# Output stores of 128-row tiles: one transfer with a three-dimensional destination in place of two

## The chip, the cores and the metric

The kernel runs on one core of one Trainium2 chip. The metric is device time in microseconds (us), the median of several runs; lower is better. A profile is one further execution, recorded instruction by instruction, with its own span (first to last instruction).

Engines are named as the profile names them: PE (matmul), PEld (PE's weight loads), DVE, ACT, POOL and SP. SP, ACT and POOL start DMA transfers from their instruction queues (SPq, ACTq, POOLq). 16 DMA engines move the data.

## The reference

Attention with a squared ReLU in place of the softmax, and a mixture of low-rank adapters on its output:

```python
scores = (1 / sqrt(64)) * q @ k.T              # q, k, v: 8 batches, 12 heads, 448 rows, 64 wide, f32
attn   = maximum(scores, 0) ** 2 / 448
x      = (attn @ v)                            # heads side by side: x is 3584 x 768
logits = x @ w_gate                            # 8 experts, the best two are kept
w      = softmax of the two kept logits
out    = x + sum over the two: w_e * (x @ A_e) @ B_e      # rank 16
```

The output is 3,584 x 768 float32, 11.01 MB.

## The kernel before

**Tiling.** The attention runs over 8 batches and, in each, three groups of four heads. The 448 rows of a batch are seven blocks of 64 that are strided: block j holds rows j, j+7, j+14 and so on, since a load reads `(p j)` with j inner. For every batch, group and block, PE makes scores (L449, `qk`), ACT or DVE applies the ReLU (L468, L470), DVE squares (L485), PE multiplies with v (L516, `pv`), and ACT or DVE copies the result to `xt` in SBUF as bfloat16 (L544). `xt` holds the transposed x for all 3,584 columns.

**Outputs.** The 3,584 rows make 28 tiles of 128, each two neighbouring blocks of 64. A batch has seven blocks, so tiles 3, 10, 17 and 24 have their first block in one batch and their second in the next. Tiles are gated in groups of three (`gate`, L560 to L639); then `outputs` works on each tile `tl` in two halves of 384 columns: PE makes x and the adapters' part in PSUM (L705 and L714, `b`), ACT or DVE evicts it to the tile's SBUF buffer `osb` (L743, `o`), and a store sends `osb` to `out`. There are four `osb` buffers. For tiles 15 to 23, x comes back by DMA transposes of `xt` into `xb` (L655), issued on SP's queue between the stores, and DVE adds it during the eviction (L734).

**Stores.** `k.out` is the output seen as `b j p f`: batch, block, row within the block, column. A row of 768 float32 is 3,072 bytes, and rows of one block lie 7 x 3,072 bytes apart. `st` (L752) walks over the tile's 128 rows and issues one transfer for each block of 64. Tiles 24 and 26 are stored from ACT's queue, all others from SP's. The last tile, 27, is stored in two halves of 384 columns, one from SP and one from ACT. That is 58 transfers.

**Loads.** q, k and v are loaded by POOL's queue, two transfers of 64 partitions for each tensor, batch and group (L185); a load casts float32 to bfloat16, so a row reads 1,792 bytes and writes 896.

**Order.** The text `ORDER` lists every operation by a short name, with the engine after a colon and the first PSUM bank after an @ sign. `ordered` turns it into the program; each engine gets its instructions in that order, and the framework adds the waits that the data, the buffers and the banks need. In the text `st` is a store (st2 is tile 1), `xb` a transpose of `xt`, `f` a load or another operation without a name of its own.

Of the kernel before, what the change touches and what calls it, by code (L numbers as in the profile page):

```python
# [14 lines left out]
J = 7  # L15
CUT = 3
SPIN = 8
PH = 64
# [11 lines left out]
PARTS = {b: ((0, S, 1),) for b in range(NB)}  # L30
PARTS.update({7: ((0, 320, 1), (320, 448, 4))})


C = dict(late=6, xi=(), om=(), merge_x=0, sqs=(2, 2, 3), xback=(15, 23), xblat=1.4, xbdur=1.35, bx=8, xlag=6, xh=2, apart=3, apcap=1, gl=(3, 1), tqlat=2.0)
# [5 lines left out]
f4 f3 f1 f0 f2 f6 f5 f8 f7 f11 f9 f10 f84@0 f12 f88 f85@2 f90 f89 f13 f87@4 qk0@6 f91 qk1@0 qk2@2 relu0:D qk3@4  # L40
f14 relu1:A relu2:D relu3:A tp2@6 f17 qk4@0 relu4:A te2 qk5@4 qk6@2 sq2 relu5:A tp3@6 f16 f86@0 relu6:A te3 sq0
qk7@0 f15 qk8@4 qk9@6 relu7:A tp4@2 relu8:D relu9:A f18 qk10@0 te4 qk11@4 relu10:A qk12@6 sq4 tp5@2 relu11:A f19
qk13@0 relu12:A te5 tp6@4 f26 relu13:A sq9 qk14@2 qk15@6 tp7 relu14:A f23 sq7 pv0@0 pv1 pv2 relu15:A pv3 qk16@2
te6 pv4 pv5 relu16:A f20 pv6 qk17@6 x13:D pv7@4 relu17:A qk18@2 sq11 pv8 f22 pv9 x12:A qk19@6 relu18:A pv10
qk20@0 relu19:D f21 pv11 relu20:A pv12 pv13 qk21@2 x27:A sq16 qk22@6 f27 qk23@0 relu21:A aw1@5 sq14 relu22:A f33
relu23:A x26:D qk24@2 tp8@6 ae1 f25 relu24:A qk25@0 sq18 qk26@4 tp9 relu25:A f55 pv14@2 pv15 pv16 relu26:A pv17
te8 qk27@0 pv18 f31 pv19 relu27:A pv20 sq23 qk28@4 qk29@6 x41:A f28 qk30@0 relu28:A x40:D aw0@3 sq25 relu29:A
f29 relu30:A qk31@4 tp10@6 ae0 tp11 relu31:A f32 sq21 qk32@0 qk33@2 relu32:A te10 pv21@4 pv22 f30 relu33:A pv23
qk34@0 sq30 qk35@6 relu34:A qk36@2 f37 relu35:D relu36:A qk37@0 pv24 pv25 pv26 relu37:A sq32 qk38@2 f35 tp12@6
pv27 relu38:A tp13 qk39@0 x55:A te12 f43 qk40@2 x54:A z0@5 relu39:A sq35 qk41@6 f34 z1 relu40:A qk42@0 relu41:D  # L50
z2 relu42:A qk43@2 f38 gmax0 relu43:A tp14@6 sq28 qk44@0 tp15 relu44:A f42 qk45@2 gd0 gu0 te14 relu45:A qk46@0
gt0 relu46:A f50 sq39 qk47@6 pv28@2 pv29 pv30 gsg0 pv31 relu47:A qk48@0 f24 pv32 pv33 gw0 sq44 pv34 relu48:A f48
qk49@6 x69:A gzp0 tp18@0 relu49:A tp19 sq37 f36 pv35@4 zt0@3 zt1 zt2 x68:A qk50@6 te18 zT0:A pv36 f41 pv37
relu50:A qk51@2 pv38 sq46 pv39 relu51:A pv40 qk52@0 f47 qk53@6 pv41 relu52:A tp16@2 x82:D tp17 relu53:A te16
qk54@0 b2@4 relu54:A sq49 f44 qk55@6 o2:A qk56@2 qk57@0 relu55:A relu56:D b0@4 f49 x83:A relu57:D qk58@6 o0:A
qk59@2 relu58:A z3@5 z4 f39 sq51 relu59:A qk60@0 qk61@6 z5 sq56 relu60:A b4@4 f40 relu61:A gmax3 qk62@2 sq58
b1@0 relu62:A f46 gu3 gd3 o4:A qk63@6 gt3 sq42 qk64@2 gsg3 o1:A b3@1 f65 relu63:A gw3 b5@4 gzp3 relu64:A sq60
f51 zt3@0 zt4 zt5 o3:A pv42@6 pv43 o5:A qk65@2 st2 pv44 zT3:A pv45 sq53 qk66@4 relu65:A pv46 pv47 pv48 tp20@0
relu66:A st4 qk67@2 tp21 x96:D x97:A f53 te20 pv49@4 relu67:A pv50 qk68@6 st0 pv51 pv52 relu68:A pv53 sq63 f66
pv54 pv55 qk69@0 qk70@2 x110:A relu69:D qk71@6 f45 relu70:A b6@4 relu71:A x111:D qk72@0 o6:D tp22@2 relu72:A  # L60
sq65 qk73@6 tp23 pv56@4 pv57 relu73:A f74 qk74@0 te22 pv58 pv59 relu74:A pv60 qk75@6 f79 pv61 sq67 pv62 relu75:A
qk76@2 b8@0 relu76:A x124:D qk77@6 f64 x125:A sq70 tp24@2 relu77:A tp25 qk78@4 z6@1 te24 f59 relu78:A qk79@6 z7
relu79:A o8:D qk80@4 qk81@2 f52 sq72 z8 relu80:A b10@0 relu81:A gmax6 sq77 f54 qk82@6 tp26@4 o10:A tp27 qk83@2
relu82:A gd6 gu6 b7@0 te26 f56 relu83:A qk84@6 gt6 o7:D qk85@4 gsg6 relu84:A qk86@2 gw6 f70 sq74 b9@0 relu85:A
pv63@6 pv64 relu86:A gzp6 pv65 qk87@4 pv66 sq79 pv67 relu87:A pv68 pv69 zt6@1 zt7 x139:A x138:D zt8 qk88@2 o9:A
qk89@4 zT6:D qk90@6 relu88:A st8 relu89:D tp28@0 tp29 relu90:A qk91@2 f80 te28 pv70@4 pv71 relu91:A pv72 pv73
qk92@6 f60 sq84 pv74 pv75 relu92:A pv76 qk93@0 b14@2 x153:D x152:A f58 relu93:A sq81 qk94@6 tp30@4 o14:A tp31
pv77@0 relu94:A pv78 f77 qk95@2 te30 pv79 pv80 relu95:A pv81 qk96@6 pv82 f57 sq91 pv83 relu96:A qk97@4 b11@2
relu97:D x166:A f67 b12@3 x167:A o11:A sq93 qk98@6 o12:A st10 qk99@0 qk100@4 relu98:A relu99:D b13@2 relu100:A
z9@3 st6 sq88 qk101@6 o13:A tp32@0 qk102@4 relu101:A tp33 b15@2 st12 f62 sq86 relu102:A qk103@6 o15:A te32 f61  # L70
qk104@4 relu103:A z10 z11 sq100 relu104:A qk105@0 f69 pv84@6 pv85 pv86 relu105:A gmax9 qk106@4 pv87 sq95 f72
pv88 relu106:A pv89 pv90 qk107@0 x181:A qk108@4 f63 gd9 gu9 x180:A relu107:D b16@2 relu108:A gt9 qk109@6 o16:D
f81 pv91@0 gsg9 pv92 relu109:A gw9 pv93 sq105 qk110@4 pv94 pv95 relu110:A pv96 f78 qk111@6 gzp9 pv97 relu111:A
x195:D zt9@2 zt10 qk112@4 sq98 x194:A zt11 f75 b17@3 relu112:A zT9:D qk113@6 o17:A sq102 pv98@0 qk114@4
relu113:A pv99 st16 tp36@2 pv100 tp37 relu114:A pv101 qk115@6 te36 pv102 pv103 relu115:A st14 pv104 tp34@4 tp35
f83 sq109 qk116@2 x209:A qk117@6 x208:A b20@1 relu116:A f68 te34 b22@0 relu117:A f71 sq114 o20:A qk118@2 qk119@4
qk120@6 relu118:A b21@1 f73 sq112 o22:A b23@2 relu119:A o21:D z12@3 sq107 relu120:A st20 qk121@0 qk122@4
relu121:A z13 relu122:D z14 o23:A qk123@6 pv105@0 gmax12 pv106 relu123:A qk124@4 gd12 pv107 gu12 pv108 gt12
sq116 pv109 relu124:A pv110 pv111 qk125@6 f82 b18@2 gsg12 relu125:A gw12 x223:D x222:A qk126@4 f76 o18:D qk127@6
relu126:A b19@1 gzp12 sq121 relu127:A zt12@0 zt13 zt14 qk128@2 pv112@4 pv113 o19:D relu128:A qk129@6 pv114  # L80
zT12:D pv115 st18 pv116 relu129:A pv117 sq123 pv118 tp38@2 qk130@0 x236:A tp39 qk131@6 st22 relu130:A b24@4 te38
relu131:A tp42@0 sq119 tp43 x237:A qk132@2 b25@6 relu132:A te42 xb90 b28@7 o24:A o25:A sq128 xb93 qk133@2 o28:A
qk134@4 tp40@0 relu133:A sq126 pv119@6 tp41 pv120 relu134:A pv121 xb91 qk135@2 te40 pv122 pv123 relu135:A pv124
pv125 qk136@4 x251:D xb94 qk137@0 x250:A b29@2 sq130 relu136:A b26@3 st24 relu137:A sq135 o29:A qk138@6 qk139@4
o26:A qk140@0 xb92 z15@2 relu138:A relu139:D z16 z17 relu140:A qk141@6 st28 gmax15 pv126@4 pv127 relu141:A gd15
pv128 gu15 qk142@0 gt15 sq133 pv129 pv130 gsg15 pv131 relu142:A xb108 qk143@6 pv132 gw15 b27@3 gzp15 x264:A
x265:D relu143:A zt15@2 xb111 zt16 zt17 sq137 pv133@0 o27:A qk144@4 tp44@6 zT15:A pv134 tp45 relu144:A xb95
qk145@2 pv135 te44 pv136 relu145:A pv137 qk146@4 pv138 pv139 st26 sq140 relu146:A z18@6 b30@7 x279:A sq142 z19
x278:A xb109 qk147@2 qk148@4 qk149@0 o30 relu147:A z20 sq144 b32@7 relu148:A xb112 relu149:A b33@2 gmax18 xb110
qk150@4 o32 qk151@0 relu150:A b31@3 gu18 o33 relu151:A gd18 qk152@4 sq149 st32 b34@7 relu152:A gt18 o31 gsg18  # L90
qk153@0 qk154@4 gw18 o34 relu153:A b35@2 st30 gzp18 relu154:A qk155@0 o35 pv140@6 relu155:A pv141 sq151 qk156@4
xb113 pv142 pv143 relu156:A qk157@2 qk158@0 pv144 pv145 relu157:D relu158:A pv146 tp46@4 tp47 x293:A x292:D
qk159@0 qk160@2 relu159:A zt18@7 te46 zt19 xb126 zt20 z21@6 relu160:A z22 sq156 zT18:A qk161@0 qk162@4 qk163@2
relu161:A xb129 b40@7 sq147 relu162:A z23 sq158 relu163:A qk164@0 xb127 pv147@4 pv148 pv149 relu164:A pv150
qk165@2 o40 pv151 pv152 relu165:A pv153 sq154 qk166@0 xb130 b41@7 relu166:A gmax21 x307:A gu21 qk167@2 gd21
pv154@0 sq163 x306:A pv155 pv156 st34 relu167:A pv157 pv158 qk168@4 gt21 o41 pv159 gsg21 pv160 b36@2 gw21 x320:A
gzp21 xb128 x321:A b38@3 sq161 relu168:A zt21@7 zt22 sq165 zt23 qk169@0 st40 zT21:A pv161@4 pv162 pv163
relu169:A pv164 qk170@6 o38 pv165 pv166 relu170:A o36 pv167 xb131 b37@3 x335:D x334:A sq168 qk171@0 qk172@6
relu171:A qk173@4 z24@2 o37 z25 relu172:A sq170 st36 b46@3 relu173:A b47@0 o46 b39@1 sq172 b44@3 o47 z26 o39
pv168@6 st46 pv169 pv170@4 gmax24 pv171 x338:A pv172@0 gd24 gu24 pv173 x343:A gt24 x339:A o44 b45@6 gsg24 x346:A  # L100
# [830 lines left out]
```

## Time and profile before

| | us |
|---|---|
| median of 3 runs | 182.09 |
| lowest and highest | 181.49 and 182.18 |
| the profiled execution's own time | 182.88 |
| its span | 180.8 |

The stages of the span, with the busy time of the engines:

| stretch, us | PE | DVE | ACT | POOL | what runs |
|---|---|---|---|---|---|
| 0 to 60 | 50.91 | 52.59 | 53.00 | 52.85 | loads at their densest, attention, no store yet |
| 60 to 120 | 58.53 | 58.83 | 59.48 | 37.09 | loads, attention and the first stores |
| 120 to 165 | 44.89 | 44.24 | 41.28 | 0 | last attention, transposes of xt, stores |
| 165 to 181 | 10.89 | 7.95 | 2.69 | 0 | outputs and stores of the last tiles |

How to read the lines shown further on. The first part of the page gives an engine's busy time, its share of the span and the number of instructions. The chain is the work that ended last, followed backwards from the last instruction; it gives shares of the span. The part on queues gives packets, megabytes and the time that the packets took as a share of 16 DMA engines over the span (q0 is POOL's queue, q1 SP's, q10 ACT's). A line of a tile's view gives the issues of a kind with their shortest, median and longest duration in ns, and when the first and the last started. A line of stretches gives, for each engine, busy time and instructions, then PE's granted clock, the mean busy share of the DMA engines, and GB/s. A line of groups gives count, busy time and mean ns, then the idle time before and what ended it.

### The profile page before, as it was taken

What the parts mean: (1) busy time and instruction counts of PE and PEld (TensorE: products, weight loads), DVE (VectorE), ACT (ScalarE), POOL (GpSimd) and SP (SyncE); (2) the same over time, 40 slices, a digit from 0 to 9 for tenths busy, and PEclk for the clock granted to TensorE, in tenths of its full rate; (3) what the DMA queues carried; (4) which work ended last, traced back from release to release, by engine and by line L of the source; (5) the groups of instructions that cost most, each with busy time, mean ns of one, the idle gap of its engine ahead of it and who ended that gap; (6) DMA issues with size and microseconds to landing.
All of it is one profiled execution on the core that took longest, in us unless ns stands there. A gap on an engine that the chain in (4) does not pass through costs nothing.

```text
span 180.8 us, 7744 instructions
## 1 busy us (share of the span) xinstructions
PE 165.2 (91%) x3366; PEld 99.2 (55%) x3366; DVE 163.6 (90%) x254; ACT 156.4 (87%) x240; POOL 89.9 (50%) x155
## 2 busy tenths in 40 slices
PE   7777889788999999999999899999999999999990
PEld 2434466454555565655646475655666557676640
DVE  0799799999989999999999899999999999999740
ACT  3499899999999999999999999999999899992120
POOL 7998998979669377760877487340000000000000
PEclk9997899999999999999999999999999999999999
DMA  5999999999999999996599999997376579467875
GB/s 94 127 175 180 156 142 179 182 184 164 214 142 146 186 237 194 176 178 141 68 143 287 224 181 259 224 170 202 68 126 144 131 175 110 101 149 176 227 215 172
DMA packets 34450, 30.50 MB, mean 169 GB/s; under 512 B 11952, under 2 KB 30896, under 8 KB 34416
## 3 DMA queue, kind: packets, MB, share of 16 engines
q0 software_dynamic: 22000, 17.03, 64.9%
q1 hardware_dynamic: 11792, 11.90, 26.5%
q10 hardware_dynamic: 624, 1.08, 2.2%
q8 instruction: 26, 0.43, 1.0%
q14 instruction: 8, 0.07, 0.1%
HBM read 33.84 MB, written 11.01 MB: 248 GB/s over the span
## 4 chain that ended last, share of the span: by engine, by line
PE 51%; ACT 27%; POOL 7%; DMA 6%; issue 4%; DVE 3%; ACTq 0%; DVEq 0%; POOLq 0%
ACT a L468 24%; PE ps L714 18%; PE ps L449 11%; PE ps L516 10%; DMA q<-in_q_dram 6%; PE ps L560 4%; PE ps L310 3%; PE ps L705 3%; POOL q L185 3%; POOL k L185 3%; PE ps L622 2%; ACT osb L743 2%; DVE a L485 2%; ACT xt L544 1%; POOL k_rest L216 1%
## 5 line engine op out<-in xcount | busy, mean ns | idle before, releaser
L468 ACT ACTIVATE a<-ps 128x896 bf16<-128x896 f32 (+3 forms) x158 | 132.6, 952 | 3.7 <-PE ps L449 3.1
L485 DVE TENSOR_TENSOR a<-a 128x1792 bf16<-128x1792 bf16 (+3 forms) x75 | 89.0, 1200 | 0.0
L449 PE MATMUL ps<-qT 64*64 64x448 bf16 (+2 forms) x756 | 58.1, 342 | 3.9 <-ACT a L468 2.4
L714 PE MATMUL ps<-B,zT 128*128 128x384 f32 x112 | 47.5, 515 | 0.0
L516 PE MATMUL ps<-a,v 64*64 64x448 bf16 (+2 forms) x756 | 45.3, 335 | 1.6 <-DVE a L485 1.3
L449 PEld LDWEIGHTS <-qT 64*64 64x64 bf16 x756 | 25.1, 105 | 31.8 <-issue 23.2
L185 POOL DMA_DIRECT2D k<-in_k_dram x46 | 27.9, 629 | 18.2 <-PE ps L310 7.3
L185 POOL DMA_DIRECT2D v<-in_v_dram x48 | 29.0, 629 | 6.2 <-PE ps L449 1.8
L185 POOL DMA_DIRECT2D q<-in_q_dram x48 | 29.4, 651 | 4.9 <-DMA v<-in_v_dram 2.7
L516 PEld LDWEIGHTS <-v 64*64 64x64 bf16 x756 | 22.7, 108 | 9.0 <-issue 4.1
L324 DVE COPY qT<-ps 128x1792 bf16<-128x1792 bf16 x21 | 22.8, 1085 | 0.2
L544 ACT CAST xt<-ps 128x448 bf16<-128x448 f32 (+2 forms) x37 | 19.0, 554 | 2.9 <-PE ps L516 2.7
L743 ACT COPY osb<-ps 128x384 f32<-128x384 f32 x26 | 13.1, 523 | 7.1 <-PE ps L714 4.1
L714 PEld LDWEIGHTS ps<-B,zT 128*128 128x128 f32 x112 | 17.3, 190 | 3.3 <-issue 0.3
L470 DVE TENSOR_SCALAR a<-ps 128x896 bf16<-128x896 f32 (+1 forms) x16 | 16.9, 1067 | 0.5 <-PE ps L449 0.5
L310 PEld LDWEIGHTS <-q 64*64 64x64 bf16 x672 | 10.4, 111 | 6.3 <-issue 2.5
L560 PEld LDWEIGHTS <-xt 128*128 128x128 bf16 x168 | 10.5, 98 | 5.8 <-issue 4.7
L560 PE MATMUL ps<-awg,xt 128*128 128x136 bf16 x168 | 13.5, 223 | 0.0
L705 PEld LDWEIGHTS <-xt 128*128 128x128 bf16 x114 | 8.0, 98 | 9.9 <-issue 8.1
L310 PE MATMUL ps<-identb,q 64*64 64x64 bf16 x672 | 10.8, 196 | 2.5 <-DMA q<-in_q_dram 1.3
L705 PE MATMUL ps<-identb,xt 128*128 128x128 bf16 x114 | 12.7, 220 | 0.2
L544 DVE CAST xt<-ps 128x448 bf16<-128x448 f32 (+2 forms) x17 | 9.6, 571 | 2.2 <-PE ps L516 2.2
(47 smaller groups left out, 97.5 us busy)
## 6 DMA issues: line engine op xcount, KB each, us to landing
out_dram<-osb SPq DMA_DIRECT2D x50, 192.0 KB, 3.9
q<-in_q_dram POOLq DMA_DIRECT2D x48, 112.0 KB, 4.8
v<-in_v_dram POOLq DMA_DIRECT2D x48, 112.0 KB, 5.0
k<-in_k_dram POOLq DMA_DIRECT2D x46, 112.0 KB, 5.1
out_dram<-osb ACTq DMA_DIRECT2D x4, 192.0 KB, 2.9
B<-in_moe_B_dram POOLq DMA_DIRECT2D x1, 384.0 KB, 8.0
xb<-xt SPq DMA_TRANSPOSE x18, 3.1
a_raw<-in_moe_A_dram POOLq DMA_DIRECT2D x1, 192.0 KB, 5.2
```

The source lines that it names most:

```text
L185: nc.gpsimd.dma_start(out=t[g * PH : g * PH + PH], in_=k.qkv[w][b, g, :, 2 * q : 2 * q + 2, :])
L310: nc.tensor.transpose(k.ps_b[sl * PH : sl * PH + PH, o.banks[g], (w * J + j) * PH : (w * J + j) * PH + PH], source(w, j)[r, sl], k.identb[ ...
L324: nc.vector.tensor_copy(t.rearrange("p g w x -> p g (w x)"), k.ps_b[:, m.banks[0] : m.banks[0] + 2, : 2 * S])
L449: nc.tensor.matmul(out=bank(o, sl)[g * PH : g * PH + PH, at : at + w], lhsT=t[r, g, 1, j * PH : j * PH + PH], rhs=t[r, g, 0, x0:x1], start ...
L468: nc.scalar.activation(out, flat(qk_ops[n], w), ACTF.Relu, scale=k.relu_scale)
L470: nc.vector.tensor_scalar(out, flat(qk_ops[n], w), k.relu_scale, 0.0, op0=ALU.mult, op1=ALU.max)
L485: nc.vector.tensor_mul(a, a, a)
L516: nc.tensor.matmul(out=bank(head, g)[sl * PH : sl * PH + PH, :w], lhsT=vn[r, sl, j * PH : j * PH + PH], rhs=T["a", g0][r, x + sl * width(n ...
L544: evac(w, lambda cp, g=g: cp(k.xt[:, g * QUADS + q, b * S + x0 : b * S + x1], bank(src, g)[:, :w]), deps=[pv_ops[n]], free=[(src, g)], key ...
L560: nc.tensor.matmul(out=bank(zops[0])[:, t * ZW : t * ZW + ZW], lhsT=k.xt[:, do, 128 * tiles[t] : 128 * tiles[t] + 128], rhs=k.awg[:, do, : ...
L705: nc.tensor.matmul(out=out(h)[:, x * 128 : x * 128 + 128], lhsT=k.xt[:, 3 * h + x, c0 : c0 + 128], rhs=k.identb, start=(x == 0), stop=Fals ...
L714: nc.tensor.matmul(out=o, lhsT=T["zT", g0][:, zi], rhs=rhs, start=xb is not None, stop=True, skip_group_check=True,)
```

## The change

A tile whose two blocks lie in one batch is stored by one transfer: its source is the whole tile of 128 partitions, its destination the two blocks, `k.out[b0, j0 : j0 + 2]`, which is a pattern of 2 blocks x 64 rows x 768 columns. A tile that lies in two batches keeps its two transfers. The halves of tile 27 become one transfer each (2 x 64 x 384).

```diff
+        (b0, j0), (b1, j1) = (divmod((c0 + r) // PH, J) for r in (0, PH))
+
         def st(e, c1=0, c2=2 * W):
-            r = 0
-            while r < 128:
-                b, x = divmod(c0 + r, S)
-                j, p = divmod(x, PH)
-                m = min(PH - p, 128 - r)
-                if b >= c["bx"]:
-                    j = TURNED[j]
-                {"SP": nc.sync, "ACT": nc.scalar, "POOL": nc.gpsimd}[e].dma_start(
-                    out=k.out[b, j, p : p + m, c1:c2], in_=T["osb", tl][r : r + m, c1:c2])
-                r += m
+            dma = {"SP": nc.sync, "ACT": nc.scalar}[e].dma_start
+            if b0 == b1:
+                dma(out=k.out[b0, j0 : j0 + 2, :, c1:c2], in_=T["osb", tl][:, c1:c2])
+                return
+            for i, (b, j) in enumerate(((b0, j0), (b1, j1))):
+                dma(out=k.out[b, j, :, c1:c2], in_=T["osb", tl][i * PH : i * PH + PH, c1:c2])
```

The text `ORDER` is written anew. Each engine's sequence of operations, and the sequence of stores and transposes on SP's queue, is the same as before; the words of different engines are interleaved otherwise, and many banks have other numbers. Of 308 takings of a bank, 19 follow another holder than before: six pairs of neighbouring score and transpose takings are exchanged, and so are seven takings among the outputs of the last tiles (b49, b50, b51, b53, b54, b55, zt27):

```diff
-gd27 gu27 o52:A gt27 gsg27 b50@4 gw27 gzp27 o53:D zt27@3 b51@2 st53 b48@5 o51:D b49@0 o50:A o48:D zT27:A st50
-b54@1 o49:A st49 b55@7 o54:D st54 o55:D st55
+z27@0 b52@1 o43 gmax27 st42 gd27 gu27 b53@3 gt27 o52:A gsg27 b50@2 gw27 gzp27 o53:D zt27@4 b51@5 st53 o50:A
+b48@3 o51:D zT27:A st50 b49@2 o48:D b54@3 o49:A st49 b55@2 o54:D st54 o55:D st55
```

The diff also brings options that are left empty here (`om2`, `fl`, `gf`, `sp`, and `sqp`, `tg`, `ai` with the values that were fixed before) and other cost figures for the planner that once made the order; none of them changes an instruction.

## The prediction

> **What bounds the kernel now.** I read the busy shares first, then the chain that ended last, then the DMA queues, then the waits of SP's queue, and last the stretches in which stores run.
>
> ```profile
> PE 165.2 (91%) x3366; PEld 99.2 (55%) x3366; DVE 163.6 (90%) x254; ACT 156.4 (87%) x240; POOL 89.9 (50%) x155
> PE 51%; ACT 27%; POOL 7%; DMA 6%; issue 4%; DVE 3%; ACTq 0%; DVEq 0%; POOLq 0%
> ```
>
> Three engines are busy for some nine tenths of the span, and the chain runs through PE and ACT. The 6% of DMA in it is the first load of q; no store stands in the chain. So today stores cost nothing but the last one's landing: the last eviction is over at 176.5 us (0.56 us from 175.92) and the span ends at 180.8.
>
> ```profile
> L760 SPq DMA_DIRECT2D out_dram<-osb x52: 466/588/1845, 61.9 to 176.2; - x52
> L760 ACTq DMA_DIRECT2D out_dram<-osb x6: 473/575/626, 171.7 to 177.0; - x6
> DMA to landing us min/median/max: 2.6/3.4/7.7
> ```
>
> 58 stores leave between 61.9 and 177.0 us, each 0.59 us of issue. SP is not short of time: it waits for its work, as the longest wait in SP's own list shows.
>
> ```profile
> SPq L760 <- ACT osb L743: 85.5, 4, 60.7
> ```
>
> The queues say how much of the 16 DMA engines the stores take, and how they are spread.
>
> ```profile
> q0 software_dynamic: 22000, 17.03, 64.9%
> q1 hardware_dynamic: 11792, 11.90, 26.5%
> q10 hardware_dynamic: 624, 1.08, 2.2%
> ```
>
> q10 is ACT's queue. Its 624 packets are 512 rows (one 64-row load, four stores of 64 rows, two half stores of 64) and 112 closing records. 112 is 7 x 16: each of its seven transfers closed on all 16 engines, so a 64-row store puts 4 rows on each. The same count fits the loads. The price of bytes on one engine is also here: 2.2% of 16 x 180.8 us is 63.6 us for 1.08 MB, 0.18 us for a 3,072-byte row, with the waiting for other queues in it. The trace's packet records give the undisturbed value: 119 ns at the least, and a row each 0.12 us where a ring has its engine for itself.
>
> ```profile
> 62.00:83.00 21.00, 20.48 (x483) 12.31 (x475) 20.94 (x31) 21.00 (x32) 13.05 (x22) 1.00 1.12 192
> 106.00:124.00 18.00, 17.96 (x438) 11.12 (x428) 17.63 (x26) 17.87 (x28) 9.05 (x16) 1.00 1.12 218
> 133.00:148.00 15.00, 15.00 (x247) 8.67 (x250) 14.59 (x32) 14.05 (x24) 0.00 (x0) 1.00 0.65 138
> ```
>
> The number before the last is the DMA share. It is about one while loads run, so no DMA engine has room then; after the loads it is 0.65.
>
> ```profile
> L185 POOL DMA_DIRECT2D v<-in_v_dram x26 | 15.6, 614 | 5.0 <-PE ps L449 1.8 <-DMA q<-in_q_dram 1.7 <-DMA k<-in_k_dram 0.6
> L185 POOL DMA_DIRECT2D q<-in_q_dram x18 | 10.9, 626 | 3.1 <-DMA v<-in_v_dram 2.7 <-DMA k<-in_k_dram 0.3
> L185 POOL DMA_DIRECT2D k<-in_k_dram x18 | 10.8, 612 | 14.4 <-PE ps L310 7.3 <-PE ps L449 6.9
> ```
>
> Those are the loads issued from 62 to 131 us: 62 of them are still to come when the first store leaves.
>
> **The change, part by part.** *Issues.* Tiles 3, 10, 17 and 24 straddle two batches and keep two transfers. The other 23, and the two halves of tile 27, lose one issue each: 58 become 33. That is 25 x 0.59 = 15 us of queue time, 23 issues of it on SP, which idles anyway: worth nothing. On ACT the store of tile 26 (two issues from 171.66 us) held up the eviction o50, and the last half is two issues ending at 177.6; one fewer there could end the run some 0.5 us sooner.
>
> *Banks.* Every engine's instructions stay in their order, but 19 of 308 bank takings follow another holder. Twelve are swaps inside a pair of score or transpose takings, and only exchange the waits of neighbours. In the tail b49, b54 and b55 now wait for the evictions o50, o48 and o49. By the rows of before o48 (173.32 plus 0.56) is over at 173.88 and b54's first matmul starts at 173.99; o49 is over at 174.67 and b55 starts at 174.85. b49 starts at 173.12 and o50 ends at 173.50, 0.4 us too late, but one issue fewer ahead of it on ACT brings it to 172.9. So zero, and 0.4 us if that issue isn't saved; behind b49 stand b54, b55 and the last stores. The cover is the half tile of matmuls (0.87 us) between two takings.
>
> *Bytes and landing.* The bytes and rows are the same. What is new is the shape: a destination of 2 x 64 rows against a source of 128 partitions, where both sides had 64. No row of before shows how a transfer whose outermost count is 2 is divided. The ends are all 16 engines (8 rows each, 1.0 us by 0.12 us a row) and two engines, one for each index of that dimension: 64 rows each, 64 x 0.12 = 7.7 us. I take two, because the only division that any transfer here shows, q10's seven, is an equal cut of an outermost count that 16 divides on both sides, and of a count of 2 such a cut gives two shares; for a finer one the engine would have to cut the next dimension, which nothing shows.
>
> The Trainium skill has a rule against this change. "DMA: Bandwidth & Descriptors", in the section "Why a DMA increments its semaphore by 16 and not by 1", says that the number of engines is the largest up to 16 that divides the slowest count of both access patterns, and its "Rules for kernel authors" say that an outermost size under 16 confines the whole transfer to that many engines. By it 128 against 2 is two engines, the lowest-numbered two each time, and the sum is the one below. The same list also advises one 128-partition transfer in place of two halves, as they share the engines anyway; by that line alone the time would be that of the first rival. No run shown so far decides between the two.
>
> *The sum with two engines.* All merged stores go through the same two engines, so their work is counted there, from the first store. 24 tiles (23, and tile 27 as two halves) x 64 rows x 0.12 = 184 us. Four straddling tiles, eight transfers of 4 rows on each engine: 8 x 4 x 0.12 = 4 us. Loads: 62 x 128 rows over 16 engines is 8 rows each, 496 rows. By the page a packet of q0 takes 64.9% of 16 x 180.8 us over 22,000, 0.085 us; as the share goes to 1.12, they overlap a little: 0.08, so 40 us. Transposes: the records show 6,912 pieces of 18 ns, 432 on an engine: 8 us. First store issued 61.9 plus 0.6 to its first row: 62.5. Together 62.5 + 184 + 4 + 40 + 8 = 298.5, and about 1.5 from the last row to the span's end (179.3 to 180.8 in before): a span of 300. The profiled execution had a span of 180.8 and a time of 182.88; the median is 182.09, 1.3 over the span. Forecast **301 us**.
>
> Why nothing hides it: from 62.5 to 177 us there are 115 us for 236 us of work. With only four osb buffers, the eviction of tile t+4 waits until tile t has landed; it stands in the order of ACT or DVE, the relus behind it wait, and then PE's scores. Loads wait too, since each has an eighth of its rows on those two engines, and alternate there with the stores; so do the transposes, on which DVE's additions from tile 15 on wait. The point from which this decides: on n engines a store's share is 24 x 128 x 0.12 / n = 369/n us, and beside 40 and 8 us of other work 115 us leave 67, so under about 5.5 engines.
>
> *Ends.* If loads, transposes and landing gaps cost nothing and a row takes 119 ns: 62.5 + 183 + 1.5 + 1.3 = 248. If a row takes 0.18 us, the mean of q10 with its waits, which then stand for the loads: 24 x 64 x 0.181 = 278, in all 62.5 + 278 + 1.5 + 1.3 = 343. I take the value near the undisturbed row plus the loads on their own, since with 14 engines idle between there is little else to wait for.
>
> **Rivals.** *Divided over 16 engines, nothing on the path (the other side).* For it: the builder may be free to cut 2 x 64 as 128 rows, as it keeps the same rows in the same order. Then landing grows from the second half's 3.4 us by at most the 0.5 us of four more rows, less the issue saved. Tail minus 0.5 us: 181.6 us. Chance 0.12. It decides wherever the cut reaches six engines or more. *The same, with the gain in ACT's tail in full:* o50 one issue (0.6 us) earlier and one issue (0.6 us) less at the end: 182.09 - 1.2 = 180.9. Against it: PE's b matmuls, 0.87 us each half tile, and not ACT, carry the chain's last 5 us. Chance 0.03. *Four engines:* 92 us of store rows, 62.5 + 92 + 4 + 40 + 8 + 2.8 = 209. Nothing speaks for a four but the chance of a cut I don't know: 0.02. *That the merge doesn't happen* is out: the built program's list of instructions has 23 stores of 2x64x768, two of 2x64x384 and the straddlers' eight of 64x768.
>
> **How the numbers follow.** Two engines 0.83, four 0.02, sixteen 0.15. Half a per cent, 0.9 us, is what the runs can tell (the three of before spread over 0.7 us). Slower: 0.85. Faster by over 0.5%: 0.03 of the tail case and 0.01 of the first rival, 0.04. Within: 0.11. The range is that of the forecast's own ends, 248 to 343; it leaves out the sixteen and four, 0.17.
>
> **What would show it.** Right: merged stores close with 2 records in place of 16, so q1 has 11,792 - 23 x 16 - 23 x 14 = 11,102 packets (11,424 if they close on sixteen); issue to landing over 8 us against 3.4; waits of ACT and DVE at the evictions for out_dram; the mean DMA share after the first store falls while the span grows; nothing changes before 62 us. Wrong: landing near 4 us and a span near 180. Right in kind but wrong in size: if the two engines serve loads first, or the transposes leave the two engines idle while DVE waits for them.

## The result and the profile after

The changed kernel takes **306.76 us** (median of 6 runs, 306.56 to 308.36), the kernel before 182.09 us (6 runs beside it, 181.49 to 182.99). The ratio is 1.687, with a 95% interval of 1.6812 to 1.6929: slower by over two thirds. The forecast was 301 us with a range of 248 to 343. Here and below, executions more than 1.5% above the fastest of their kernel are left out of the ratios, though not of the medians; two stood far above, one of the kernel before (299.91 us) and one of experiment 7's second kernel (373.93 us).

The page after, its busy shares, the three rows on the clock and the DMA engines in 40 slices, the queues, and the chain that ended last:

```profile
PE 193.5 (63%) x3366; PEld 109.3 (36%) x3366; DVE 164.9 (54%) x254; ACT 159.6 (52%) x240; POOL 90.2 (30%) x155
...
PEclk9799999999758995997775797975897986555755
DMA  6999999989664786666762196992195111111211
...
q0 software_dynamic: 22000, 17.03, 40.7%
q1 hardware_dynamic: 11102, 11.90, 25.2%
q10 hardware_dynamic: 564, 1.08, 1.1%
...
DMA 11%; DVE 0%; DVEq 0%; issue 0%
DMA out_dram<-osb 11%; DVE osb L770 0%; DVEq L952 0%; DVEq L770 0%
```

No engine is near nine tenths of the span any more. DVE, ACT and POOL do the work of before in nearly the same busy time; PE does the same 3,366 matmuls in 193.5 us where it had 165.2, at a granted clock of 0.804 in the mean (0.988 before), lowest where PE waits most. The queues move the same bytes. q1 has 690 packets fewer: 23 merged stores close with 2 records in place of 32 (23 x 30 = 690). The chain that ended last, 51% PE before, is now a store: 34.6 us from 254.5 us on, then DVE's last eviction. In the DMA row a lone 1 or 2 is two of sixteen engines at work.

The tile view of `osb`, whose columns for an issue are the shortest, median and longest duration in ns:

```profile
L784 SPq DMA_DIRECT2D out_dram<-osb x23: 511/544/7906, 62.0 to 289.7; - x23
L787 SPq DMA_DIRECT2D out_dram<-osb x6: 532/588/9702, 108.5 to 228.9; - x6
...
  DMA out_dram<-osb: 84.2, 11
```

The first store leaves at 62.0 us as before (61.9), and in the 60 us before it each engine's busy time is within 2% of what it was (PE 50.43 us against 50.91). The evictions into `osb` idle 84.2 us for earlier stores; before, that row did not exist.

The waits of the whole span (us in all, times, longest):

```profile
ACT osb L770 <- DMA out_dram<-osb: 49.5, 6, 13.1
...
ACT a L471 <- PE ps L452: 38.2, 28, 5.5
DVE osb L770 <- DMA out_dram<-osb: 32.9, 4, 13.2
...
PEld L313 <- DMA q<-in_q_dram: 15.3, 14, 3.3
...
DVE osb L761 <- DMA xb<-xt: 12.7, 2, 8.1
```

A full `osb` holds ACT and DVE in their order for up to 13 us at a time; besides, PE's transposes of q wait for their loads, the additions for `xb`, and the ReLUs for PE's scores.

Stretches of the span (engine busy times, then PE's granted clock, DMA share, GB/s):

```profile
62.00:83.00 21.00, 15.02 (x417) 9.61 (x406) 16.54 (x24) 15.02 (x21) 8.88 (x15) 0.93 0.79 128
66.00:106.00 40.00, 26.14 (x563) 14.69 (x555) 24.07 (x34) 24.44 (x35) 15.14 (x26) 0.83 0.67 109
255.00:279.00 24.00, 5.75 (x16) 2.90 (x17) 1.48 (x4) 1.23 (x4) 0.00 (x0) 0.50 0.13 52
```

The last of them is the plainest line of the trace. A share of 0.13 is 2.1 engines of 16, and 52 GB/s is what they moved: 26 GB/s each. The packet records of the same 24 us hold 407 store rows of 3,072 bytes, 0.118 us a row on each of two engines. Of these rows 128 are ACT's, the store of tile 26 that was issued at 259.7 us; they are sent among SP's, from 263.7 us on, and the rate stays that of two engines. So the merged stores of both queues go through the same two, as the prediction's sum assumed. In the stretch from 66 to 106 us they hold 437 store rows and 3,278 load rows. That is 5.5 store rows per us on each of the two engines, and 5.1 load rows on each of sixteen, if the loads are spread evenly: about one for one.

### The profile page after: what moved, and what is told of

Its sections match the earlier page's. It is cut to its first block, busy times and chain, and to the rows that moved or that the text cites. A ratio compares the mean times of both kernels' runs of the same rounds, so it can differ in the third digit from the quotient of the medians.

```text
span 305.6 us, 7703 instructions
## 1 busy us (share of the span) xinstructions
PE 193.5 (63%) x3366; PEld 109.3 (36%) x3366; DVE 164.9 (54%) x254; ACT 159.6 (52%) x240; POOL 90.2 (30%) x155
## 3 DMA queue, kind: packets, MB, share of 16 engines
q1 hardware_dynamic: 11102, 11.90, 25.2%
## 5 line engine op out<-in xcount | busy, mean ns | idle before, releaser
L734 PE MATMUL ps<-B,zT 128*128 128x384 f32 x112 | 57.9, 614 | 15.1 <-DVE osb L761 15.0
L452 PE MATMUL ps<-qT 64*64 64x448 bf16 (+2 forms) x756 | 63.4, 368 | 5.2 <-ACT a L471 2.7
L519 PE MATMUL ps<-a,v 64*64 64x448 bf16 (+2 forms) x756 | 53.1, 372 | 7.9 <-DVE osb L761 3.9
L770 ACT COPY osb<-ps 128x384 f32<-128x384 f32 x26 | 12.6, 502 | 53.0 <-DMA out_dram<-osb 49.5
L519 PEld LDWEIGHTS <-v 64*64 64x64 bf16 x756 | 25.5, 120 | 20.0 <-issue 13.0
L725 PE MATMUL ps<-identb,xt 128*128 128x128 bf16 x114 | 14.6, 245 | 26.2 <-ACT osb L770 14.2
L770 DVE COPY osb<-ps 128x384 f32<-128x384 f32 x12 | 6.6, 555 | 44.9 <-DMA out_dram<-osb 32.9
L734 PEld LDWEIGHTS ps<-B,zT 128*128 128x128 f32 x112 | 21.0, 228 | 19.4 <-DVE osb L761 15.5
L761 DVE TENSOR_TENSOR osb<-ps,xb 128x384 f32<-128x384 f32 x18 | 9.7, 552 | 33.3 <-issue 18.5
L725 PEld LDWEIGHTS <-xt 128*128 128x128 bf16 x114 | 9.2, 109 | 40.1 <-issue 39.0
L313 PE MATMUL ps<-identb,q 64*64 64x64 bf16 x672 | 12.6, 205 | 12.9 <-DMA q<-in_q_dram 11.2
```

Of the source, the lines that this page charges most:

```text
L313: nc.tensor.transpose(k.ps_b[sl * PH : sl * PH + PH, o.banks[g], (w * J + j) * PH : (w * J + j) * PH + PH], source(w, j)[r, sl], k.identb[ ...
L452: nc.tensor.matmul(out=bank(o, sl)[g * PH : g * PH + PH, at : at + w], lhsT=t[r, g, 1, j * PH : j * PH + PH], rhs=t[r, g, 0, x0:x1], start ...
L519: nc.tensor.matmul(out=bank(head, g)[sl * PH : sl * PH + PH, :w], lhsT=vn[r, sl, j * PH : j * PH + PH], rhs=T["a", g0][r, x + sl * width(n ...
L725: nc.tensor.matmul(out=out(h)[:, x * 128 : x * 128 + 128], lhsT=k.xt[:, 3 * h + x, c0 : c0 + 128], rhs=k.identb, start=(x == 0), stop=Fals ...
L734: nc.tensor.matmul(out=o, lhsT=T["zT", g0][:, zi], rhs=rhs, start=xb is not None, stop=True, skip_group_check=True,)
L770: cp(osb()[:, h * W : h * W + W], out(h)[:, :W])
```

## The experiments

Each ran beside the kernel before on the same chip, whose medians in the four sets were 181.69 us (experiments 1 to 3), 182.12 (4, 5 without the sixteen, and the six tiles of 7), 182.61 (6 with four buffers, and the first set of 7's two tiles) and 181.36 (the rest).

**1. The change without its merge.** New `ORDER`, new banks, two transfers for every tile.

```diff
-            if b0 == b1:
-                dma(out=k.out[b0, j0 : j0 + 2, :, c1:c2], in_=T["osb", tl][:, c1:c2])
-                return
```

> The changed kernel with its two transfers of 64 rows put back for every tile; its new order text and banks stay. Theory (two DMA engines carry each merged store): 182.1 us, within 0.9, q1 again 11,792 packets, stores landing in about 4 us. Rival (the bank takings that follow another holder, or the rewritten order, cost something): 185 us or more, with waits at the last b matmuls.

181.35 us (12 runs), ratio 0.9994 (0.9963 to 1.0024). q1 has 11,792 packets and stores land in 3.3 us at the median. The whole slowdown comes with the merged transfers; order and banks are worth nothing that can be measured.

**2. The merge, with 64 as the outermost count.** The same number of transfers, the same rows in each, the destination written as 64 x 2 rows.

```diff
-                dma(out=k.out[b0, j0 : j0 + 2, :, c1:c2], in_=T["osb", tl][:, c1:c2])
+                dma(out=k.out[b0, j0 : j0 + 2, :, c1:c2].rearrange("j p f -> p j f"), in_=T["osb", tl][:, c1:c2])
```

> The changed kernel with the two dimensions of the merged destination exchanged: 64 x 2 rows in place of 2 x 64, still one transfer of 128 rows of 3,072 bytes to the same two blocks; the rows of a tile go to each other's places in the output. Theory (the outermost count alone sets the number of engines): 16 closing records for each merged store, q1 11,424 packets, landing about 4 us, 181.1 to 182.5 us. Rival (a transfer of twice the size is what blocks the queue and the buffers): 8 us or more to land and 250 us or more, as in the changed kernel.

181.52 us (12 runs), ratio 1.0001 (0.9961 to 1.0041). Its page and the tile view of `osb`:

```profile
q1 hardware_dynamic: 11424, 11.90, 22.6%
...
out_dram<-osb SPq DMA_DIRECT2D x22, 384.0 KB, 3.6
```

```profile
L784 SPq DMA_DIRECT2D out_dram<-osb x23: 538/554/1338, 62.8 to 177.2; - x23
...
DMA to landing us min/median/max: 2.7/3.4/7.6
```

The packets are those that the prediction gave for a close on sixteen engines, 11,424, and landing is that of before. So neither three dimensions nor 384 KB in one transfer cost anything: the outermost count of 2 does. The run also shows what a merge is worth where it is spread well: 25 issues fewer, and no time gained.

**3. The gain at the end alone.** The kernel before, with only the halves of tile 27 stored by one 64 x 2 transfer each. The last copies of x are written with the two blocks' columns interleaved, so that every row keeps its place in the output.

```diff
+        last = (b, u) == (NB - 1, 1)
+
+        def two(x):
+            return x.rearrange("p (r j) -> p j r", j=2) if last else x
+
+        def one(x):
+            return x.rearrange("p (j r) -> p j r", j=2) if last else x
...
-            evac(w, lambda cp, g=g: cp(k.xt[:, g * QUADS + q, b * S + x0 : b * S + x1], bank(src, g)[:, :w]),
+            evac(w, lambda cp, g=g: cp(two(k.xt[:, g * QUADS + q, b * S + x0 : b * S + x1]), one(bank(src, g)[:, :w])),
...
+            if tl == NT - 1:
+                {"SP": nc.sync, "ACT": nc.scalar}[e].dma_start(
+                    out=k.out[NB - 1, J - 2 : J, :, c1:c2].rearrange("j p f -> p j f"), in_=T["osb", tl][:, c1:c2])
+                return
```

> The kernel before, with only tile 27's two half stores merged, as 64 x 2 rows: the last copies of x write their 128 columns interleaved, so that row r of that tile is row r//2 of block 5 + r%2, and the output is in place. One issue of some 0.6 us fewer at the end of SP's and of ACT's queue. Theory: 181.6 us, 0.5 under the kernel before, since the last issue of before (177.03 us) is gone and the one at 176.51 closes the run. Rival (the eviction, and the landing of twice the rows, set the end): 182.1 us, no change.

181.74 us against 181.69 (12 runs), ratio 1.0009 (0.9983 to 1.0035). No gain can be told: the interval leaves room for 0.3 us at most, and the 0.5 us of the theory lies outside it. That speaks for the rival.

**4. Late buffers, or too few bytes per time?** A store that lands late can be covered by more buffers; two engines that are busy without a break can't. The changed kernel with seven `osb` buffers in place of four:

```diff
-POOLS = dict(qT=5, a=11, zp=2, zT=3, osb=4, w=3, q=5, k=5, v=8, xb=3)
+POOLS = dict(qT=5, a=11, zp=2, zT=3, osb=7, w=3, q=5, k=5, v=8, xb=3)
```

> The changed kernel with seven osb buffers in place of four. Theory (the two engines have 236 us of rows to move after 62.5 us, whatever waits for them): 297 to 307 us. Rival (each store's own landing is too long for four buffers, so evictions wait for latency): more stores in flight hide it, under 260 us.

307.16 us (2 runs), ratio 1.687 (1.675 to 1.698), the same as with four. Its waits:

```profile
ACT a L471 <- PE ps L452: 55.7, 20, 13.6
DVE qT L327 <- PE ps L313: 36.4, 6, 13.8
PEld L313 <- DMA q<-in_q_dram: 28.7, 12, 12.3
```

The wait of the evictions has all but gone (6.2 us, once, against 84.2). It has become PE's wait for q, and ACT's and DVE's wait for PE. The 84 us of waits for a buffer in the changed kernel are where the delay shows, not what makes it.

**5. Four, eight and sixteen engines.** All 28 tiles by one transfer each, with an outermost count c of 4, 8 or 16 (`rows` is the output as 3,584 x 768, set by one more line, `h.rows = out`):

```diff
-            if b0 == b1:
-                dma(out=k.out[b0, j0 : j0 + 2, :, c1:c2], in_=T["osb", tl][:, c1:c2])
-                return
-            for i, (b, j) in enumerate(((b0, j0), (b1, j1))):
-                dma(out=k.out[b, j, :, c1:c2], in_=T["osb", tl][i * PH : i * PH + PH, c1:c2])
+            dma(out=k.rows[128 * tl : 128 * tl + 128, c1:c2].rearrange("(r c) f -> c r f", c=4),
+                in_=T["osb", tl][:, c1:c2])
```

> Each of the 28 tiles is stored by one transfer with 4 x 32 rows: tile t's rows fill rows 128t to 128t+127 of the output, row r at place 4 (r mod 32) + r // 32, so the rows are in other places than the reference's. Theory (as many engines as the outermost count): four engines have 28 x 32 x 0.12 = 107 us of stores beside 40 of loads and 8 of transposes from 62.5 us on, 221 us in all, 215 to 230. Rival (a destination of three dimensions always goes to two engines): 28 x 64 x 0.12 = 215 us of stores, 328 us. Rival (the place of rows in memory is what was slow in the changed kernel, and these rows lie close together): 182 us.

> The same with 8 x 16 rows. Theory: eight engines have 28 x 16 x 0.12 = 54 us of stores, 102 us with loads and transposes, in the 115 us there are: 182 to 188 us, since an engine's work almost fills the time. Rival (what counts is the landing of each store, which is twice that of sixteen engines): 190 us or more.

> As e4_outer4 and e5_outer8, rows of tile t at 128t to 128t+127 of the output, but 16 x 8 rows for each transfer. Theory (the outermost count, not the place of the rows, made those two slow): 180.8 to 183.5 us. Rival (rows close together in memory cost something themselves, which would explain why those two came out above what was expected): 186 us or more.

The three pages, in this order:

```profile
q1 hardware_dynamic: 11064, 11.90, 22.3%
```

```profile
q1 hardware_dynamic: 11168, 11.90, 24.2%
```

```profile
q1 hardware_dynamic: 11376, 11.90, 24.9%
```

SP issues 26 transfers in each, and 52 in the kernel before, so what is left of q1 without closing records is 11,792 - 52 x 16 = 10,960. The three counts are 10,960 plus 26 x 4, 26 x 8 and 26 x 16 to the packet, and that of experiment 2 is 10,960 plus 29 x 16: a store goes over as many engines as its outermost count has indices, up to sixteen. The DMA share says the same where stores are all that is left: 0.26 of 16 engines, 4.2, in the run with four (220 to 226 us). The Trainium skill states the rule in "DMA: Bandwidth & Descriptors", section "Why a DMA increments its semaphore by 16 and not by 1", as the largest number up to 16 that divides the slowest counts of both sides; the counts 2, 4, 8, 16 and 64 agree with it, but as powers of two they can't tell it from the count itself, capped at 16.

| outermost count | engines by q1 | median us | ratio | last load row, us | expected us |
|---|---|---|---|---|---|
| 2 (the change) | 2 | 306.76 | 1.687 (1.681 to 1.693) | 172.5 | 301 |
| 4 | 4 | 249.62 (2 runs) | 1.371 (1.361 to 1.380) | 154.8 | 215 to 230 |
| 8 | 8 | 202.82 (4 runs, 198.39 to 205.72) | about 1.09, by its fastest run | 134.4 | 182 to 188 |
| 16 | 16 | 182.55 (10 runs) | 1.0072 (1.0033 to 1.011) | 121.8 | 180.8 to 183.5 |

Sixteen held; for eight and four the time expected was too low. For eight the rival, each store's landing, has the number (190 or more), but in its trace the evictions idle only 4.4 us for stores. The last load row, from the packet records, says where: it is 12.6 us later with eight engines than with sixteen, and 33.0 us later with four. Twelve stores leave in that time. With eight engines each puts 8 more rows on every engine that it uses, 12 x 8 x 0.12 = 11.5 us; with four, 24 more rows, 12 x 24 x 0.12 = 34.6 us. So in these two runs the loads are delayed by about the full time of the rows that are too many. It is no general rule: the same sum gives 67 us for the change (ten merged stores before the last load row, 56 rows more on each of the two engines), and 49.8 were measured; experiment 6 shows 13 of 20. The rest is lost after the last load: spans of 203.6 and 247.9 against 180.2 are 23.4 and 67.7 us more, 10.8 and 34.7 of them there. (The trace with eight is of the longest of the four executions, 205.72 us; the shortest, 198.39, took 7 us less, so its 10.8 may be much smaller.) With four engines, the waits from 60 to 250 us name the buffers and the loads:

```profile
PEld L313 <- DMA q<-in_q_dram: 14.5, 5, 7.8
...
DVE osb L770 <- DMA out_dram<-osb: 13.5, 3, 6.4
```

**6. Merged stores in the load phase alone.** Only tiles 0, 1 and 2 by one 2 x 64 transfer, first with four and then with seven `osb` buffers:

```diff
-            if b0 == b1:
+            if tl in (0, 1, 2):
```

> The changed kernel with only tiles 0, 1 and 2 merged (2 x 64), the first three stores, from 62 us on, while loads fill every DMA engine; all others as two transfers. Theory (during the loads no engine has room, so each row more on the two engines is added to the load phase): 3 x 56 rows x 0.12 = 20 us later for the last load row (143 in place of 122 to 124), less the 4 to 6 us that engines stand idle about 84 us; 196 to 203 us. Rival (only the sum over the run counts: 20 us in the 67 that are spare until the end): 182 to 184 us.

> The kernel of e9_first3 (tiles 0 to 2 merged) with seven osb buffers in place of four. Theory (the loads that share the two engines come late): still 193 to 198 us. Rival (the eviction of a later tile waits for a buffer whose store hasn't landed, which is the 12.2 us that ACT waits for out_dram in e9_first3): 182 to 186 us, and that wait gone.

195.69 us, ratio 1.081 (1.071 to 1.091), and 195.99 us, ratio 1.083 (1.076 to 1.090). Three stores cost 13 to 15 us. Their last load rows come at 135.0 and 135.8 us. The 143 expected of the first was too late, and its time ends just under the range; the rival, that only the sum over the run counts (182 to 184), is out. So is the second's rival: the wait for the buffer has gone, and the time has not. The same stretch in the kernel before, in the first and in the second kernel:

```profile
83.00:100.00 17.00, 16.37 (x367) 9.78 (x363) 16.68 (x22) 16.54 (x26) 10.68 (x18) 1.00 0.86 163
```

```profile
83.00:100.00 17.00, 11.83 (x204) 6.01 (x203) 8.94 (x12) 11.21 (x17) 4.39 (x9) 0.78 0.56 104
```

```profile
83.00:100.00 17.00, 4.35 (x96) 2.72 (x96) 2.11 (x3) 2.02 (x4) 4.07 (x8) 0.60 0.57 103
```

And the longest wait for a DMA in the first and in the second:

```profile
ACT osb L770 <- DMA out_dram<-osb: 12.2, 2, 9.8
```

```profile
PEld L313 <- DMA q<-in_q_dram: 15.3, 6, 12.8
```

The DMA share and the GB/s are the same in both, though the engines wait for other things. With four buffers ACT waits for a store; with seven it runs on, uses up the loads that are there, and then everything stands 12.8 us for q. The wait for the buffer had only hidden a wait for a load of about its size.

**7. Merged stores after the loads.** Six tiles spread over the run (1, 5, 9, 13, 16 and 20), and then only the two of them that leave among the transposes. The second of these kernels ran in two sets; its trace is of the second.

```diff
-            if b0 == b1:
+            if tl in (1, 5, 9, 13, 16, 20):
```

```diff
-            if b0 == b1:
+            if tl in (16, 20):
```

> The changed kernel with only tiles 1, 5, 9, 13, 16 and 20 merged (2 x 64), all others as two transfers of 64 rows. Theory (throughput of the two engines): 6 x 64 x 0.12 = 46 us, the other 22 tiles 21, loads 40, transposes 8: 115 us in the 115 there are, so 182 to 192 us. Rival (every merged store holds its buffer for 8 us or more and the engines wait for it): six times some 6 us, 215 us or more.

> The changed kernel with only tiles 16 and 20 merged (2 x 64), both stored after the last load and each with a transpose of xt right behind it on SP's queue; all others as two transfers. Theory (a transpose lands only after the 64 rows ahead of it on the two engines, and DVE waits for it in order): the load phase ends as before (about 123 us), the transpose behind tile 20 lands some 8 us later than 3, DVE shows waits for xb, and the time is 186 to 196 us. Rival (2 x 7.7 us of rows fit in engines that have a third of their time free there): 182 to 184 us, no wait for xb.

> The kernel of e10_two_late once more, for its profile. Theory (the transpose behind a merged store lands late and DVE waits for it): 191 to 194 us again, last load as in the kernel before, and DVE's additions from tile 18 on waiting for xb or for an osb buffer, 5 to 12 us in all. Rival (PE's clock alone, which fell in other runs, makes the time): no such wait, PE's busy time longer by some 10 us.

Six tiles: 209.47 us (4 runs, 207.55 to 214.40), ratio 1.140 (1.133 to 1.148) by the two fastest, between the two expectations and so for neither. Two tiles: 192.53 us, ratio 1.059 (1.050 to 1.068), and 192.85 us, ratio 1.064 (1.054 to 1.074). The time is in the range of the theory, and the rival of 182 to 184 is out: two stores of 28 cost 10 to 11.5 us, at a time when the DMA engines have a third of their time free. Before them nothing is changed: the last load row is at 121.8 us. In the tile view of `xb`, the landing of the transposes in the kernel before, and then the transposes of this one:

```profile
DMA to landing us min/median/max: 2.3/3.1/4.5
```

```profile
L674 SPq DMA_TRANSPOSE xb<-xt x18: 1199/1256/3697, 122.6 to 161.2; - x18
...
DMA to landing us min/median/max: 2.3/3.3/11.1
```

and among its waits, and in the stretch after the loads in the kernel before and the two stretches of this one:

```profile
DVE osb L761 <- DMA xb<-xt: 5.0, 1, 5.0
```

```profile
123.00:181.00 58.00, 52.78 (x926) 33.11 (x924) 49.19 (x97) 41.07 (x75) 0.00 (x0) 0.99 0.66 151
```

```profile
60.00:123.00 63.00, 61.65 (x1329) 36.47 (x1331) 62.02 (x87) 62.52 (x94) 37.09 (x63) 1.00 1.06 193
123.00:191.50 68.50, 57.13 (x920) 34.89 (x908) 48.68 (x96) 40.70 (x74) 0.00 (x0) 0.91 0.64 125
```

The longest landing of a transpose was 4.5 us before and is 11.1 now, as it must be if transposes have pieces on the two engines that still have a merged store's rows to send. DVE then waits 5.0 us for `xb`, which it did not before, and PE 4.1 us behind it. PE's clock after 123 us is 0.91 where it was 0.99, and its busy time over the run is 170.0 us against 165.2; the rival had 10 us more and no wait. The wait is shown; of the 10 to 11.5 us it explains five at most, and how the rest divides between the waits behind it and the slower clock was not separated.

## Why the prediction was right, point by point

**Two engines: right, and it is the whole cause.** 11,102 packets were named for it and counted, and the share of 0.13 shows two engines at work, the same two for both queues. The sign "landing over 8 us" can't be read, since the views give no landing for the merged stores. Experiments 1 and 2 leave nothing for the order, the banks, the size of a transfer or its third dimension.

**The sum: right within 2%, in part by luck.** It gave a span of 300 us, and 305.6 was measured. The first store row starts at 64.0, not 62.5 (63.1 in the kernel before); the last ends at 304.1, 1.5 us before the end as assumed. Between them lie 240 us, where the sum had 236. Two of its terms were a little high: a store row takes 0.118 us on its own (0.12 was taken, 3 us too much in 1,536 rows), and a load row beside it some 0.07 us (0.08 was taken, 5 us too much in 496 rows). The 0.07 is an estimate: of the 40 us from 66 to 106 us, 218 store rows take 25.8, and the rest is left for 205 load rows. Against that stand gaps, 9.7 us in all between 182 and 233 us, in which no store row is under way. The sentence that 14 idle engines leave "little else to wait for" was wrong by so much: in that stage DVE's additions wait for `xb`, and the stores come after them. That each gap is made so was not tried. The terms that were too high and the gaps that were left out nearly cancel. A reading that the sum doesn't use was wrong too: the load on q10 has 128 rows, not 64; only so do its rows add up to 512.

**Who waits: right in all three places.** Evictions for `osb` (84.2 us), loads (the last row at 172.5 us against 122.7), additions for transposes (12.7 us). The working put the buffers first. Experiments 4 and 6 show that they come second: with enough of them the time is the same, and the loads are what is waited for.

**Banks at zero, issues at nothing: right**, by experiments 1, 2 and 3. The 0.5 us that fewer issues could save at the end did not show: merging the last tile alone (experiment 3) leaves room for 0.3 us at most.

**"The point from which this decides": wrong.** The step added up the work of an engine between 62.5 and 177 us, found 67 us free, and concluded that stores on six engines or more would be hidden and on four would cost 27 us (209). Four engines cost 67 us and eight cost 16 to 24 (with 28 tiles merged in place of 24). The free time is an average over two stages. While loads run the DMA share is above one, so an engine has none, and extra rows move the loads by three fifths of their own length or more (experiments 5 and 6). After the loads there is free time, but transposes stand in the same queue with a consumer that waits: two stores were felt there although the share is 0.64 (experiment 7), in part by that wait. The forecast didn't rest on this step, since two engines are beyond it either way; the rival of four engines did, and so did the claim that the sixteen-engine case reaches down to six.

**The rivals.** The sixteen-engine case was fairly priced: 181.6 us, 0.5 under the kernel before, and the merge spread over sixteen (as 64 x 2) took 181.52 beside 181.69, no difference that can be told. Only the chip's cut was other than it supposed.

## What to carry to other kernels

Before two transfers are joined, look at the outermost count of the joined pattern on both sides, the DRAM side too: it, and not the 128 partitions, set here how many DMA engines the store used, and a pattern of the same rows with 64 outermost cost nothing. Count closing records in the queue's packets to see it. Price a transfer that is confined to few engines by its rows on one of them, stage by stage, against what the same engines have to do in that stage; the mean DMA share hides both the stage without spare time and the transfer that waits in line. And where a wait for a buffer appears, more buffers may only turn it into another wait of the same length.

## What the hardware showed besides

An issue on SP, 0.59 us before, took up to 7.9 us (9.7 for a straddling tile's) while rows of earlier merged stores were still queued, and up to 15.8 us with seven buffers: SP's queue itself stood still, with the transposes behind it.

On the engines that had both loads and stores to serve, neither came first, and rows of both went at about equal rates although they differ in length: from 66 to 106 us of the changed kernel, if loads are spread evenly, 5.5 store rows of 3,072 bytes and 5.1 load rows of 1,792 read bytes per us.

PE's granted clock followed its waits: a mean of 0.804 over the span and 0.50 from 255 to 279 us, against a mean of 0.988 before; the same matmuls were 28 us longer busy. This did not set the end here, since two DMA engines did, but may be a part of experiment 7's loss.

Sixteen as the outermost count, with a tile's 128 rows side by side in DRAM, was 0.7% slower than before (1.0033 to 1.011), with landing at 4.4 us in place of 3.4. Why was not tried.
